# Filtered products of a spectral layer stored by frequency class

## The chip, the core and the metric

The kernel runs on one core of a Trainium2 chip. The metric is the device time of one execution in microseconds, the median of several runs; 204.33 us for the kernel before (204.27 to 204.45 in three runs). A core has five engines with instruction queues of their own, which run side by side and wait for one another through semaphores: TensorE (PE in the profile, with its weight loads as PEld), VectorE (DVE), ScalarE (ACT), GpSimd (POOL) and SyncE (SP, which issues transfers here). SBUF is the on-chip memory of 128 partitions (`arena` in the profile), PSUM the memory that TensorE writes (`ps`).

## What is computed

`x` has 2048 rows of 640 columns in bf16. Cut to what matters:

```python
xn = layernorm(x)                          # over the 640 columns
X = rfft2(xn)                              # 2048 x 321 complex
y = irfft2(X * (w_r + 1j * w_i), s=(2048, 640))
h = (xn @ w_gate) * (xn @ w_up)            # 640 -> 1536
out = x + y + h @ w_down                   # 1536 -> 640
```

One half is a filter in the frequency domain, with a real and an imaginary weight for each frequency; the other is a bilinear gated layer. They share the normalised input and are added at the end.

## The kernel before

The two-dimensional transform is taken apart into small products. The 640 columns fall into ten blocks of 64; butterflies on VectorE (L887 to L925) reduce the ten blocks to five classes of frequencies, and TensorE does the rest with tables. Of the rows, 2048 are 32 times 64: one step over 32 (L938), then, for each of 32 values of `q`, a product over 64. The values of `q` are worked two at a time, in 16 steps of `t`. The way of one `q` through the middle of the kernel is:

- D (L1056): column products, five matmuls of 64 or 65 columns for each half of the pair, evicted to SBUF by ScalarE or VectorE (L718 and L719 are the copy helper that most evictions go through).
- C (L1079): the row product over 64 for one `q`, 128 x 321 in PSUM.
- WM (L1094, L1097): VectorE multiplies the 321 frequencies by `w_r` and `w_i` and writes both products as bf16 into a strip `yg` of SBUF. L1094 runs twice, once for each half (`h`) of classes 0 to 3; 2 weights x 32 frequencies x 4 classes = 256 elements in each. L1097 does class 4 by itself.
- NG (L1106, L1107): the negative of the `w_i` products of classes 0 to 3, on ScalarE, VectorE or GpSimd, as the planner chose (16, 8 and 8 of the 32).
- NS (L1114 to L1116): the copies and the negation for class 4, on GpSimd.
- IA (L1130, L1131): the inverse row product. For each of the five classes, two matmuls of 64 columns that add up in PSUM: first with the weights (`w_r` products, `w_i` products), then with (minus `w_i` products, `w_r` products). Here the filtered products are the stationary operand, so each matmul has a weight load of 128 columns.
- An eviction (L718 or L719), and when all 32 are done the inverse column product I (L1159) with butterflies on VectorE (L1183 to L1216).

Two lines say how `yg` is laid out. WM writes the classes innermost, so that the four classes of one frequency are neighbours, and IA picks one class with a step of four:

```python
dst = yg[:, 578:1090].rearrange("p (w h m k) -> p h w m k", w=2, h=2, k=4)[:, h]
l1, l2 = yg[:, 578 + k:1090:4], yg[:, 322 + k:834:4]
```

Elements 322 to 577 hold minus `w_i` products, 578 to 833 `w_r` products, 834 to 1089 `w_i` products.

The gated layer is woven into this: GU (L978 with 512 columns, L998 with fewer) is five matmuls into a bank of PSUM, evicted mostly by ScalarE, then multiplied by H on VectorE (L1014). The product with `w_down` (L1237), the last step over rows (L1249), and the sum with `x` (L1257) close the kernel.

The order of work is not written by hand: a planner in the kernel takes tasks with estimated durations, priorities and a stock of eight PSUM banks, and fixes one static order for each engine before the program is emitted. Each engine then works through its list in that order and waits where a task needs another engine's result. The estimates belong to the tasks (895 ns for a whole WM, for instance) and not to the access patterns.

Of the kernel before, what the change touches and what calls it, by code (L numbers as in the profile page):

```python
# [495 lines left out]
_ACTF = mybir.ActivationFunctionType  # L496
_OP = AluOpType
# [53 lines left out]
def _build(nc, A_x, A_w_r, A_w_i, B_w_gate, B_w_up, B_w_down, out, opts=None):  # L551
# [3 lines left out]
    with es:  # L555
# [147 lines left out]
        def bank_of(t):  # L703
            return t.units[1]
# [259 lines left out]
        for ui, (at_, ci, ft0) in enumerate(units):  # L964
            b0, nb = chunks[ci][:2]
            n = 128 * nb
# [59 lines left out]
        for t in range(16):  # L1026
            pq = 10.0 + 0.05 * t
            ar = t % 3
            yr = t % _NY
            wr = (t // (_WQ // 2)) % _NW  # L1030
            if t % (_WQ // 2) == 0:
                q0 = 2 * t
                for w_ in range(2):
                    wv, dw = wvs[w_], v_wr[wr][:, w_]
                    parts = [(dw[0:64], wv[:, q0:q0 + _WQ, :].rearrange("k1 q l -> k1 (q l)").unsqueeze(1).to_broadcast(
                        [_S1, 2, _WQ * 321]), 64 * _WQ * 642)]
                    o_ = 0
                    if q0 == 0:
                        o_ = 1
                        parts.append((dw[64:128, 0:321], wv[:, _R // 2, :].unsqueeze(1).to_broadcast([_S1, 2, 321]), 64 * 642))  # L1040
                    for d_ in range(2):
                        parts.append((dw[64 + d_:128:2, 321 * o_:321 * _WQ].rearrange("p (q l) -> p q l", l=321),
                                      wv[:, _R - q0 - o_:_R - q0 - _WQ:-1, :], 32 * (_WQ - o_) * 642))
                    for i_, (dst, src_, nb_) in enumerate(parts):
                        dma("ld_w%d_%d_%d" % (t, w_, i_), dst, src_, nb_,
                            [(b_wr[wr][0], ("r", b_wr[wr][1] + 8 * w_ + 2 * i_, b_wr[wr][1] + 8 * w_ + 2 * i_ + 2))],
                            prio=9.5 + 0.05 * t, semkey=("w", wr), after=[muls[opts.get("w_after", 15)]])

            eds = []
            for w in range(2):  # L1050
                def em_d(c, t=t, w=w):
                    bk = bank_of(c.t)
                    ins = None
                    for k in range(5):
                        n = 64 if k < 4 else 65
                        ins = c.e.matmul(ps[:, bk, k * 64:k * 64 + n], v_uq[:, k, t, :],  # L1056
                                         v_fd[:, k * 128 + w * n: k * 128 + w * n + n], start=True, stop=True)
                    return ins
                td = T("D_%d_%d" % (t, w), "pe", 5 * _d_mm(64), em_d, reads=[(b_u, None), (b_fd, None)],
                       prio=pq, bank="single", cls="b")  # L1060

                def em_ed(c, td=td, ar=ar, w=w):
                    bk = bank_of(td)
                    ins = None
                    for g in range(2):
                        ins = copy_on(c, v_a[64 * w:64 * w + 64, ar, 324 * g:324 * g + 321],
                                      ps[64 * g:64 * g + 64, bk, 0:321])
                    return ins
                ed = T("eD_%d_%d" % (t, w), ("act", "dve"), {"dve": 960.0, "act": 840.0},
                       em_ed, writes=[(b_a, ("r", 2 * ar + w, 2 * ar + w + 1))], prio=pq - 0.001, frees=td)  # L1070
                hold(td, ed)

            for g in range(2):
                q = 2 * t + g
                pg = pq + 0.0005 * g
                ys = 2 * yr + g

                def em_c(c, q=q, g=g, ar=ar):
                    return c.e.matmul(ps[:, bank_of(c.t), 0:_LP], v_tf[:, q, :], v_a[:, ar, 324 * g:324 * g + _LP],  # L1079
                                      start=True, stop=True)  # L1080
                tc = T("C_%d" % q, "pe", _d_mm(_LP), em_c, reads=[(b_a, ("r", 2 * ar, 2 * ar + 2)), (b_tf, ("t", t, t + 1))],
                       prio=pg, bank="single", cls="b")

                def em_wm(c, tc=tc, yr=yr, wr=wr, q=q, g=g):
                    bk = bank_of(tc)
                    o_ = 321 * (q % _WQ)
                    wg = v_wr[wr][:, :, o_:o_ + 321]
                    yg = v_y[:, yr, g]
                    for h in range(2):
                        xh = ps[:, bk, 0:256].rearrange("p (k h m) -> p h m k", k=4, h=2)[:, h]  # L1090
                        wv = wg[:, :, 0:320].rearrange("p w (m k) -> p w m k", k=10)
                        wv = wv[:, :, :, 1:5] if h == 0 else wv[:, :, :, 9:5:-1]
                        dst = yg[:, 578:1090].rearrange("p (w h m k) -> p h w m k", w=2, h=2, k=4)[:, h]
                        c.e.tensor_tensor(dst, xh.unsqueeze(1).to_broadcast([128, 2, 32, 4]), wv, _OP.mult)  # L1094
                    x5 = ps[:, bk, 256:321].unsqueeze(1).to_broadcast([128, 2, 65])
                    d5 = yg[:, 0:512].rearrange("p (w n) -> p w n", w=2)[:, :, 0:65]
                    return c.e.tensor_tensor(d5, x5, wg[:, :, 0:321:5], _OP.mult)  # L1097
                wm = T("WM_%d" % q, "dve", 895.0, em_wm,
                       reads=[(b_wr[wr][0], ("r", b_wr[wr][1], b_wr[wr][1] + 16))],
                       writes=[(b_y, ("r", 4 * ys, 4 * ys + 1))], prio=pg - 0.001, frees=tc)  # L1100
                hold(tc, wm)

                def em_ng(c, yr=yr, g=g):
                    yg = v_y[:, yr, g]
                    if c.e is nc.scalar:
                        return c.e.activation(yg[:, 322:578], yg[:, 834:1090], _ACTF.Copy, scale=-1.0)  # L1106
                    return c.e.tensor_scalar(yg[:, 322:578], yg[:, 834:1090], -1.0, None, _OP.mult)  # L1107
                T("NG_%d" % q, opts.get("ng_eng", ('pool', 'act', 'dve')),
                  {"act": _d_act(256), "dve": _d_dve_ts16(256), "pool": 900.0}, em_ng,
                  reads=[(b_y, ("r", 4 * ys, 4 * ys + 1))], writes=[(b_y, ("r", 4 * ys + 1, 4 * ys + 2))], prio=pg - 0.001)  # L1110

                def em_ns(c, yr=yr, g=g):
                    yg = v_y[:, yr, g]
                    c.e.tensor_copy(yg[:, 65:128], yg[:, 257:320])  # L1114
                    c.e.tensor_copy(yg[:, 193:256], yg[:, 1:64])  # L1115
                    return c.e.tensor_scalar(yg[:, 128:193], yg[:, 256:321], -1.0, None, _OP.mult)  # L1116
                T("NS_%d" % q, "pool", 700.0, em_ns,
                  reads=[(b_y, ("r", 4 * ys, 4 * ys + 1))], writes=[(b_y, ("r", 4 * ys + 2, 4 * ys + 3))], prio=pg - 0.001)

                def em_ia(c, q=q, yr=yr, g=g):  # L1120
                    bk = bank_of(c.t)
                    ins = None
                    yg = v_y[:, yr, g]
                    for k in range(5):
                        if k < 4:
                            l1, l2 = yg[:, 578 + k:1090:4], yg[:, 322 + k:834:4]
                        else:
                            l1, l2 = yg[:, 0:128], yg[:, 128:256]
                        dst = ps[:, bk, 64 * k:64 * k + 64]
                        c.e.matmul(dst, l1, v_ti[:, q, 0, :], start=True, stop=False)  # L1130
                        ins = c.e.matmul(dst, l2, v_ti[:, q, 1, :], start=False, stop=True)  # L1131
                    return ins
                ia = T("IA_%d" % q, "pe", 10 * _d_mm(64), em_ia,
                       reads=[(b_y, ("r", 4 * ys, 4 * ys + 3)), (b_wd, ("e", 128 * q, 128 * q + 128))],
                       prio=pg, bank="single", cls="b")

                def em_eia(c, ia=ia, t=t, g=g):
                    src = ps[:, bank_of(ia), 0:320].rearrange("p (k a m) -> p k a m", k=5, a=16)
                    return copy_on(c, v_z2w[:, :, :, t, 4 * g:4 * g + 4], src)
                eia = T("eIA_%d" % q, ("act", "dve"), {"dve": _d_dve_psum(320), "act": _d_act(320)}, em_eia,  # L1140
                        writes=[(b_z2, ("t", q, q + 1))], prio=pg - 0.001, frees=ia)
                hold(ia, eia)
# [207 lines left out]
```

## Time and profile before

| | |
|---|---|
| device time | 204.33 us (204.27 to 204.45) |
| span in the profile | 202.8 us |
| TensorE busy | 198.0 us (98%), 1785 matmuls |
| VectorE busy | 179.5 us (89%) |
| ScalarE busy | 127.5 us (63%) |
| GpSimd busy | 32.0 us (16%) |
| L1094, 64 instructions | 24.0 us, 416 ns each |
| weight loads of L1130 and L1131, 320 | 23.6 us, 114 and 113 ns each |
| first and last L1094 | 86.5 and 137.1 us |
| first and last L1130 | 90.0 and 139.3 us |

[...]matmuls of 64 columns are listed with 196 ns and start about 30 ns apart. So the pace is read from the starts. Weight loads overlap in the same way. On VectorE, too, an instruction is listed with its tail: two of L1094 in a row take 0.75 us together and not 0.83. A group's row gives line, engine, operation, destination and source with shapes, number of instructions, busy time and mean duration, and the idle time of the engine just ahead of them with what ended it.

### The profile page before, as it was taken

What the parts mean: (1) busy time and instruction counts of PE and PEld (TensorE: products, weight loads), DVE (VectorE), ACT (ScalarE), POOL (GpSimd) and SP (SyncE); (2) the same over time, 40 slices, a digit from 0 to 9 for tenths busy, and PEclk for the clock granted to TensorE, in tenths of its full rate; (3) what the DMA queues carried; (4) which work ended last, traced back from release to release, by engine and by line L of the source; (5) the groups of instructions that cost most, each with busy time, mean ns of one, the idle gap of its engine ahead of it and who ended that gap; (6) DMA issues with size and microseconds to landing.
All of it is one profiled execution on the core that took longest, in us unless ns stands there. A gap on an engine that the chain in (4) does not pass through costs nothing.

```text
span 202.8 us, 4769 instructions
## 1 busy us (share of the span) xinstructions
PE 198.0 (98%) x1785; PEld 128.1 (63%) x1785; DVE 179.5 (89%) x511; ACT 127.5 (63%) x277; POOL 32.0 (16%) x108
## 2 busy tenths in 40 slices
PE   7999999999999999899999999999999999999995
PEld 7987644454444555556666666667777767777774
DVE  3599999999999997697988898864999999999983
ACT  3678899999975776869999999987611220200000
POOL 0000000000000000075754675453000000000000
DMA  6999983031161597605354444004313332332222
GB/s 183 300 341 378 377 80 65 3 65 32 32 63 39 112 276 194 197 14 132 74 145 114 103 102 127 0 5 136 92 32 97 106 107 66 113 90 81 93 65 65
DMA packets 31542, 23.82 MB, mean 117 GB/s; under 512 B 10528, under 2 KB 29472, under 8 KB 31392
## 3 DMA queue, kind: packets, MB, share of 16 engines
q1 hardware_dynamic: 30720, 23.16, 43.5%
q10 hardware_dynamic: 800, 0.36, 0.6%
q8 instruction: 14, 0.23, 0.5%
q14 instruction: 8, 0.07, 0.1%
HBM read 18.92 MB, written 2.62 MB: 106 GB/s over the span
## 4 chain that ended last, share of the span: by engine, by line
PE 85%; DVE 5%; SPq 4%; DMA 4%; issue 1%; ACT 1%
PE ps L978 44%; PE ps L1237 23%; SPq L712 4%; DMA arena<-in_A_x_dram 4%; PE ps L1131 3%; PE ps L1130 3%; PE ps L998 2%; PE ps L1079 2%; PE ps L938 2%; PE ps L1159 2%; PE ps L1249 2%; PE ps L1056 2%; DVE arena L719 1%; DVE arena L1257 1%; DVE arena L1186 0%
## 5 line engine op out<-in xcount | busy, mean ns | idle before, releaser
L718 ACT ACTIVATE arena<-ps 128x512 bf16<-128x512 f32 (+7 forms) x206 | 104.8, 547 | 40.1 <-PE ps L1159 24.0
L978 PE MATMUL ps<-arena 128*128 128x512 bf16 x420 | 97.0, 379 | 0.1
L978 PEld LDWEIGHTS ps<-arena 128*128 128x128 bf16 x420 | 38.9, 98 | 41.9 <-ACT arena L718 1.4
L1237 PE MATMUL ps<-arena 128*128 128x320 bf16 (+2 forms) x396 | 56.5, 295 | 0.2 <-DVE arena L1257 0.2
L1237 PEld LDWEIGHTS ps<-arena 128*128 128x128 bf16 x396 | 37.6, 98 | 13.9 <-DVE arena L1257 0.5
L1094 DVE TENSOR_TENSOR arena<-ps,arena 128x256 bf16<-128x256 f32 x64 | 24.0, 416 | 0.1
L1014 DVE TENSOR_TENSOR arena<-arena 128x512 bf16<-128x512 bf16 x42 | 17.7, 421 | 4.7 <-ACT arena L718 4.7
L1107 POOL TENSOR_SCALAR arena<-arena 128x256 bf16<-128x256 bf16 x8 | 6.8, 855 | 89.3 <-DVE arena L1097 89.2
L719 DVE CAST arena<-ps 64x321 bf16<-64x321 f32 (+1 forms) x25 | 12.2, 490 | 6.3 <-PE ps L1131 5.8
L1257 DVE TENSOR_TENSOR arena<-ps,arena 128x320 bf16<-128x320 f32 (+2 forms) x33 | 15.4, 473 | 1.8 <-PE ps L1249 1.8
L998 PE MATMUL ps<-arena 128*128 128x128 bf16 (+1 forms) x160 | 14.4, 246 | 0.4 <-ACT arena L718 0.4
L1130 PEld LDWEIGHTS ps<-arena 128*128 128x128 bf16 x160 | 12.4, 114 | 2.8 <-ACT arena L718 0.4
L998 PEld LDWEIGHTS ps<-arena 128*128 128x128 bf16 x160 | 12.0, 98 | 2.1 <-ACT arena L718 1.2
L1130 PE MATMUL ps<-arena 128*128 128x64 bf16 x160 | 13.3, 196 | 0.0
L1131 PE MATMUL ps<-arena 128*128 128x64 bf16 x160 | 13.3, 197 | 0.0
L1131 PEld LDWEIGHTS ps<-arena 128*128 128x128 bf16 x160 | 11.2, 113 | 2.1
L1116 POOL TENSOR_SCALAR arena<-arena 128x65 bf16<-128x65 bf16 x32 | 12.1, 378 | 0.0
L1114 POOL COPY arena<-arena 128x63 bf16<-128x63 bf16 x32 | 8.6, 268 | 17.1 <-DVE arena L1097 17.0
L1097 DVE TENSOR_TENSOR arena<-ps,arena 128x130 bf16<-128x130 f32 x32 | 9.3, 292 | 0.0
L776 ACT ACTIVATE arena<-arena 128x640 bf16<-128x640 bf16 x11 | 9.1, 824 | 0.0
L1115 POOL COPY arena<-arena 128x63 bf16<-128x63 bf16 x32 | 9.0, 280 | 0.0
L891 DVE TENSOR_TENSOR arena<-arena 128x384 f32<-128x384 bf16 x16 | 8.8, 552 | 0.0
(62 smaller groups left out, 221.0 us busy)
## 6 DMA issues: line engine op xcount, KB each, us to landing
arena<-in_A_x_dram SPq DMA_DIRECT2D x20, 160.0 KB, 2.4
out_dram<-arena SPq DMA_DIRECT2D x31, 80.0 KB, 1.6
arena<-in_A_w_r_dram SPq DMA_DIRECT2D x8, 160.5 KB, 3.0
arena<-in_A_w_i_dram SPq DMA_DIRECT2D x8, 160.5 KB, 3.0
arena<-in_B_w_gate_dram SPq DMA_DIRECT2D x4, 320.0 KB, 5.8
arena<-in_A_x_dram SPq DMA_DIRECT2D x1, 1280.0 KB, 9.8
arena<-in_A_w_r_dram SPq DMA_DIRECT2D x14, 80.2 KB, 2.9
arena<-in_A_w_i_dram SPq DMA_DIRECT2D x14, 80.2 KB, 3.1
```

What stands on the lines that cost most here:

```text
L718: return c.e.activation(dst, src, _ACTF.Copy)
L719: return c.e.tensor_copy(dst, src)
L978: ins = c.e.matmul(ps[:, bk, :], v_gw[:, w, j, ft, :], v_xt[:, j, rows], start=(j == 0), stop=(j == 4))
L998: ins = c.e.matmul(ps[:, bk, w * n:(w + 1) * n], v_gw[:, w, j, ft, :], v_xt[:, j, rows], start=(j == 0), stop=(j == 4))
L1014: return c.e.tensor_tensor(v_ht[:, ft0, rows], v_gbf[:, rr, 0, :], v_gbf[:, rr, 1, :], _OP.mult)
L1094: c.e.tensor_tensor(dst, xh.unsqueeze(1).to_broadcast([128, 2, 32, 4]), wv, _OP.mult)
L1097: return c.e.tensor_tensor(d5, x5, wg[:, :, 0:321:5], _OP.mult)
L1116: return c.e.tensor_scalar(yg[:, 128:193], yg[:, 256:321], -1.0, None, _OP.mult)
L1130: c.e.matmul(dst, l1, v_ti[:, q, 0, :], start=True, stop=False)
L1131: ins = c.e.matmul(dst, l2, v_ti[:, q, 1, :], start=False, stop=True)
L1237: ins = c.e.matmul(ps[:, bk, 0:sl3.stop - sl3.start], v_ht[:, ft, a * 128:(a + 1) * 128], v_wd[:, ft, sl3], start=(ft == _FT_ORDER[0]), st ...
L1257: return c.e.tensor_tensor(v_out[:, a % 2, sl3], ps[:, bk, 0:sl3.stop - sl3.start], v_xr[:, xs, sl3], _OP.add)
```

## The change

The products of one class are put into one run of columns. The strip from 322 to 1089 keeps its size, but is now four blocks of 192, one for each class `k`, and in each block three runs of 64: minus `w_i` products, `w_r` products, `w_i` products. Both sets of weights of a class are then 128 neighbouring columns of the block, which is what the change is for: the weight load of the inverse row product reads without a step. To get there the products of WM are written with the four classes 192 elements apart, and the negation goes over four rows of 64 in place of one of 256. Class 4 is as it was.

```diff
-                        dst = yg[:, 578:1090].rearrange("p (w h m k) -> p h w m k", w=2, h=2, k=4)[:, h]
+                        dst = yg[:, 322:1090].rearrange("p (k s h m) -> p h s m k", k=4, s=3, h=2)[:, h, 1:3]
                         c.e.tensor_tensor(dst, xh.unsqueeze(1).to_broadcast([128, 2, 32, 4]), wv, _OP.mult)
...
                     yg = v_y[:, yr, g]
+                    yk = yg[:, 322:1090].rearrange("p (k s n) -> p s k n", k=4, s=3)
                     if c.e is nc.scalar:
-                        return c.e.activation(yg[:, 322:578], yg[:, 834:1090], _ACTF.Copy, scale=-1.0)
-                    return c.e.tensor_scalar(yg[:, 322:578], yg[:, 834:1090], -1.0, None, _OP.mult)
+                        return c.e.activation(yk[:, 0], yk[:, 2], _ACTF.Copy, scale=-1.0)
+                    return c.e.tensor_scalar(yk[:, 0], yk[:, 2], -1.0, None, _OP.mult)
...
                         if k < 4:
-                            l1, l2 = yg[:, 578 + k:1090:4], yg[:, 322 + k:834:4]
+                            b0 = 322 + 192 * k
+                            l1, l2 = yg[:, b0 + 64:b0 + 192], yg[:, b0:b0 + 128]
                         else:
                             l1, l2 = yg[:, 0:128], yg[:, 128:256]
```

## The prediction

> **What bounds the kernel now.** I read the chain of waits first, because only work on it can move the end. Over the stretch in which the changed lines run (86 to 137 us), its summary by line is:
>
> ```profile
> by line: PE ps L978 66.0%; PE ps L1131 9.7%; PE ps L1130 9.6%; PE ps L1079 7.5%; PE ps L1056 6.6%; DVE arena L719 1.0%; issue 0.1%
> ```
>
> TensorE holds practically all of it, so here the kernel runs at TensorE's pace; the inverse row product (L1130, L1131), which the change is to speed up, has a fifth of it. But that product's operands come from VectorE, so I next read the busy time of each engine over pieces of about 6.75 us, in which the order of work repeats (two values of t, four of q):
>
> ```profile
> core 0: us, PE busy (x) PEld busy (x) DVE busy (x) ACT busy (x) POOL busy (x), PEclk, DMA share, GB/s
> 85.10:91.95 6.85, 6.83 (x64) 3.98 (x65) 6.78 (x22) 5.09 (x13) 4.37 (x14) 1.00 0.07 19
> 91.95:98.70 6.75, 6.61 (x89) 4.14 (x87) 5.59 (x19) 6.36 (x16) 3.50 (x11) 1.00 0.37 96
> 98.70:105.46 6.76, 6.76 (x90) 4.27 (x87) 5.79 (x20) 6.46 (x16) 3.98 (x14) 1.00 0.58 148
> 105.46:112.20 6.74, 6.74 (x90) 4.25 (x87) 5.80 (x20) 6.49 (x16) 4.02 (x14) 1.00 0.38 100
> ```
>
> VectorE is full in the first piece and idle for only 0.95 us in each later one. That spare time is the number on which the forecast turns. The timeline of VectorE shows where it lies and what stands around it:
>
> ```profile
> 106.83 0.99 DVE L719 CAST arena<-ps 64x321 bf16<-64x321 f32 x2
> 108.73 0.49 DVE L719 CAST arena<-ps 128x320 bf16<-128x320 f32 x1 [0.92 <-PE ps L1131]
> 109.19 0.76 DVE L1094 TENSOR_TENSOR arena<-ps,arena 128x256 bf16<-128x256 f32 x2
> 109.87 0.30 DVE L1097 TENSOR_TENSOR arena<-ps,arena 128x130 bf16<-128x130 f32 x1
> 110.08 0.42 DVE L1014 TENSOR_TENSOR arena<-arena 128x512 bf16<-128x512 bf16 x1
> ```
>
> The only gap is one wait of 0.92 us for an inverse product; everything else on VectorE stands shoulder to shoulder. Last, the groups by shape give the durations:
>
> ```profile
> L1094 DVE TENSOR_TENSOR arena<-ps,arena 128x256 bf16<-128x256 f32 x64 | 24.0, 416 | 0.1
> ...
> L1130 PEld LDWEIGHTS ps<-arena 128*128 128x128 bf16 x160 | 12.4, 114 | 2.8 <-ACT arena L718 0.4
> ...
> L1097 DVE TENSOR_TENSOR arena<-ps,arena 128x130 bf16<-128x130 f32 x32 | 9.3, 292 | 0.0
> ...
> L1056 PEld LDWEIGHTS ps<-arena 128*128 128x128 bf16 x160 | 6.5, 98 | 0.7 <-issue 0.2
> ```
>
> A weight load with a step of four elements takes 114 ns on average, one without a step 98.
>
> **What the Trainium skill says.** (1) "Vector Engine (DVE) Microarchitecture Reference", section "5.2 Measured stream behaviour on trn2 (trn3 not measured)": a port keeps its full rate only while elements come in runs of at least two adjacent words; a destination that hops 4 KiB at every element takes 1.71 ns per column in place of 1.054, one that steps 24 words takes 2.50, and two sources that step 72/152 words take 1.75. These are for 4-byte data. No long instruction in the trace of before writes SBUF one element at a time, so it doesn't show this; it shows that runs are free (the 320-element copy on VectorE that writes runs of four bf16 took 492 ns, the 64 products 416, the same as float32 instructions of 256 elements with long runs, 415 to 421). It also speaks partly against a strict reading: L1097 reads bf16 at a step of 10 bytes, each mostly alone in its 8 bytes, and at 292 ns shows no visible penalty. (2) "SBUF — State Buffer", section "Door 1: The DMA port swizzle": lines of 16 bytes, with at least two hits in a line needed for full rate; L1097 has 1.6 a line, the new writes one. (3) "VectorE: DVE Perf Modes", section "Mode 1× (REGULAR) — the baseline": the plain mode takes "weird strides, PSUM operands — all work". The trace agrees for a PSUM source read at a step of 256 bytes (L1094 today). (4) "TensorE: Matmul & The Clock Gate", section "LDWEIGHTS (loading the stationary operand)": the time follows the number of columns. The trace differs, 114 against 98 ns at 128 columns; the measurement decides.
>
> **The change part by part.** The number and order of instructions is the same on every engine; only access patterns change, so no wait is added by the program.
>
> *The weight loads of L1130 and L1131, four of five classes.* I summed all blocks of inverse products in TensorE's timeline, start to start: 10.36 us for 320 matmuls, 32.4 ns each. The column product L1056, as narrow but with weights in one run, goes at 0.29 us for ten, 29.2 each. The change makes every block like that: 320 x 3.2 ns = 1.0 us less for TensorE, 0.13 us in each piece of 6.75. All of it is on today's path.
>
> *The products of L1094, 64 instructions of 256 elements.* The inner four elements of the destination, today adjacent (8 bytes), are put 384 bytes apart (192 elements of bf16), so each lands alone; sources and element count are unchanged. Cost per element, bounded from both sides: nothing (the trace shows no penalty for single bf16 reads at 10 bytes) up to 2.50 - 1.05 = 1.45 ns (the 24-word step). I take 1.71 - 1.054 = 0.656 ns, because that price is for a destination that goes round a few regions and returns to the next element of each, as ours goes round four classes; 256 x 0.656 = 168 ns, L1094 at some 584. An estimate, from the page's table.
>
> *The negation (L1106/L1107: 16 on ScalarE, 8 on VectorE at 250 ns, 8 on GpSimd at 855).* Its 256 elements become four rows of 64, each in one run and at an even offset. I cost it at nothing on all three, since rows of 64 are long runs.
>
> *L1097, the zero-frequency class and its copies on GpSimd (L1114 to L1116)* are untouched.
>
> **What the 168 ns do.** Behind each L1094 on VectorE stand further products, H (L1014), the negations and the evictions of L719; TensorE waits for products through the negation (0.25 to 0.86 us) and the copies on GpSimd (0.86 us together), with 0.4 to 1.1 us to spare (read off the timelines of the three engines between 104 and 112 us) before the inverse product has to start. First run of twelve (86.5 to 91.9): 12 x 0.168 = 2.0 us, less gaps of 0.30 and 0.85 up to 95.7: 0.9 late. Six pieces up to 136: each gets 8 x 0.168 = 1.34 us and has 0.95: 0.39 x 6 = 2.35 late. The last four products have 0.67 more just ahead of the last inverse products and little slack: 0.4. Sum 3.7 us. TensorE's 1.0 us gain lies in the same stretch, and there it only becomes waiting, since VectorE now sets the pace. Everything after 139 us starts later by the same amount: the butterflies of the inverse transform wait for the last inverse product, and their stage (VectorE holds the chain from 156 to 164 us) is unchanged. 204.3 + 3.7 = 208.0 us.
>
> **The rivals.** *R1, scattered writes are free, or cheap enough to hide.* For it: L1097's reads at 10 bytes and L1094's PSUM reads at 256 bytes run at full rate. Up to about 100 ns per product would vanish in the gaps ((0.30 + 0.85 + 6 x 0.95) / 60 = 0.11 us for the first 60). Then TensorE keeps its gain: 204.3 - 1.0 = 203.3. ScalarE, 6.49 of 6.74 us busy, could cap it, but 0.13 us per piece is within its 0.25 of spare time. Against it: one hit per line, which both pages price. *R2, the penalty is a whole cycle or more per element.* At one cycle (1.04 ns, an estimate between the two prices): 267 ns per product; 12 x 0.267 - 1.15 = 2.05, six times (2.13 - 0.95) = 7.1, last 0.9: 10 us, 214.4. At 2.50 ns per column: 372 ns; 3.3 + 12.2 + 1.3 = 16.8 us, 221.1. For it: the write is of two bytes, and our 384 bytes are nearer to the 24-word step than 4 KiB is. Against: the 72/152-word steps cost hardly more than 4 KiB. *R3, the penalty exists but TensorE and VectorE share it well:* the gaps take it almost wholly and gain and loss cancel, within 0.2% of before.
>
> **How the numbers follow.** Forecast 0.50; R1 0.22; R2 0.26, half of it at or below the one-cycle case; R3 0.02. The range goes from 203.2 (R1 at its full gain) to 214.5 (the one-cycle case) and leaves out the upper half of R2 and a little more, under 0.2. Faster is R1, 0.22, same is R3 with edges, 0.03, slower the rest, 0.75.
>
> **What would show it.** The mean of L1094: 584 ns is the forecast, 416 is R1, 680 or more R2. The weight loads of L1130 and L1131 should stand at 98 ns in every case, and blocks of ten inverse products at 0.29 us where TensorE doesn't wait. In the forecast VectorE has no gap left between 86 and 137 us, its wait for L1131 is gone, the pieces of 6.75 us grow to about 7.15, and TensorE's products wait for GpSimd, ScalarE or VectorE. I am wrong if L1094 does not move (then the pieces shrink to about 6.62), or if rows of 64 slow the negations.

## The result and the profile after

The changed kernel takes 251.49 us (250.16 to 252.7), beside 204.39 us for the kernel before on the same chip: a ratio of 1.230 (95% interval 1.225 to 1.234), 47.1 us slower. The direction of the forecast was right and its size far off.

The chain of waits from 83 to 140 us of the changed kernel (line numbers above L1097 have moved by up to two):

```profile
by line: DVE arena L1094 69.2%; DVE arena L719 10.1%; issue 6.2%; DVE arena L1014 4.1%; PE ps L978 3.9%; DVE arena L1097 3.7%; PE ps L1056 1.7%; PE ps L1132 0.9%; PE ps L1133 0.9%; DVE arena L1108 0.6%; PE ps L1079 0.3%
```

VectorE has taken the path over from TensorE, and over two thirds of it are the products. The groups by shape:

```profile
L1094 DVE TENSOR_TENSOR arena<-ps,arena 128x256 bf16<-128x256 f32 x64 | 78.2, 1413 | 1.5 <-PE ps L1079 1.4
...
L1097 DVE TENSOR_TENSOR arena<-ps,arena 128x130 bf16<-128x130 f32 x32 | 16.1, 504 | 0.0
...
L1132 PEld LDWEIGHTS ps<-arena 128*128 128x128 bf16 x160 | 12.0, 104 | 35.3 <-ACT arena L718 19.2 <-issue 7.6 <-DVE arena L1014 3.4
...
L1107 ACT ACTIVATE arena<-arena 128x256 bf16<-128x256 bf16 x16 | 6.7, 417 | 39.9 <-DVE arena L1097 39.9
```

L1094 went from 416 to 1413 ns. L1097 was not touched and is listed with 504 in place of 292: it starts at 108.34 in the timeline below, before the two products ahead of it end (106.27 + 2.46 = 108.73), so a listed duration tells less than the step from start to start. That step is in the same timeline of VectorE:

```profile
105.66 0.49 DVE L719 CAST arena<-ps 128x320 bf16<-128x320 f32 x1 [2.03 <-PE ps L1133]
106.27 2.46 DVE L1094 TENSOR_TENSOR arena<-ps,arena 128x256 bf16<-128x256 f32 x2
108.34 0.51 DVE L1097 TENSOR_TENSOR arena<-ps,arena 128x130 bf16<-128x130 f32 x1
108.76 0.41 DVE L1014 TENSOR_TENSOR arena<-arena 128x512 bf16<-128x512 bf16 x1
```

Two L1094 and one L1097, all the products of one q, take 108.76 - 106.27 = 2.49 us; in the lines of before it is 110.08 - 109.19 = 0.89. With 0.21 for L1097, one L1094 takes 1.14 us of VectorE's time (before 0.34): 0.80 us more, 3.1 ns for each of 256 elements. Before, an element took about 1.05 ns, an estimate: 0.34 us for the 256 of L1094 and 0.21 for the 130 of L1097 make 0.13 us for 126 elements, and some 70 ns are left for each instruction. A lone bf16 so comes to about 4.2 ns in all.

Busy time of the engines in pieces of four q, which now last 12.25 us in place of 6.75:

```profile
core 0: us, PE busy (x) PEld busy (x) DVE busy (x) ACT busy (x) POOL busy (x), PEclk, DMA share, GB/s
101.00:106.27 5.27, 4.39 (x43) 2.87 (x44) 3.11 (x8) 2.47 (x6) 0.87 (x3) 0.54 0.15 35
106.27:118.55 12.28, 7.84 (x86) 4.10 (x85) 12.23 (x19) 6.93 (x16) 4.04 (x13) 1.00 0.21 54
118.55:130.78 12.23, 7.61 (x85) 4.07 (x84) 12.19 (x20) 6.71 (x16) 4.04 (x13) 1.00 0.33 83
```

In the second and third row VectorE has no gap left (12.23 of 12.28), and TensorE is busy for less than two thirds. In the first row the granted clock of TensorE is 0.54, and it works at about half speed: in the chain, five matmuls of L978 take 2.23 us there, 1.08 before. That has a part in VectorE's wait of 2.03 us for L1133 at 105.66. The same wait before was shorter:

```profile
95.23 0.49 DVE L719 CAST arena<-ps 128x320 bf16<-128x320 f32 x1 [0.85 <-PE ps L1131]
```

What lowers the clock there no run isolates.

### The profile page after: what moved, and what is told of

The parts are those of the page before. It is cut to its first block, busy times and chain, and to the rows that moved or that the text cites. A ratio compares the mean times of both kernels' runs of the same rounds, so it can differ in the third digit from the quotient of the medians.

```text
span 249.8 us, 4769 instructions
## 1 busy us (share of the span) xinstructions
PE 212.2 (85%) x1785; PEld 130.4 (52%) x1785; DVE 230.4 (92%) x511; ACT 129.0 (52%) x277; POOL 32.7 (13%) x108
## 4 chain that ended last, share of the span: by engine, by line
PE 50%; DVE 37%; issue 4%; SPq 3%; DMA 3%; POOL 1%; ACT 1%; POOLq 0%
DVE arena L1094 27%; PE ps L978 23%; PE ps L1239 19%; DVE arena L719 4%; SPq L712 3%; DMA arena<-in_A_x_dram 3%; PE ps L998 2%; PE ps L938 2%; DVE arena L1014 2%; PE ps L1161 2%; DVE arena L1097 2%; PE ps L1251 2%; PE ps L1056 1%; PE ps L1132 0%; POOL arena L1117 0%
## 5 line engine op out<-in xcount | busy, mean ns | idle before, releaser
L978 PE MATMUL ps<-arena 128*128 128x512 bf16 x420 | 104.2, 399 | 7.0 <-DVE arena L1097 6.9
L1094 DVE TENSOR_TENSOR arena<-ps,arena 128x256 bf16<-128x256 f32 x64 | 78.2, 1413 | 1.5 <-PE ps L1079 1.4
L978 PEld LDWEIGHTS ps<-arena 128*128 128x128 bf16 x420 | 40.2, 101 | 53.6 <-DVE arena L1097 8.6
L1239 PEld LDWEIGHTS ps<-arena 128*128 128x128 bf16 x396 | 37.6, 98 | 13.9 <-DVE arena L1259 0.5
L1132 PE MATMUL ps<-arena 128*128 128x64 bf16 x160 | 14.9, 202 | 24.2 <-ACT arena L718 12.0
L1132 PEld LDWEIGHTS ps<-arena 128*128 128x128 bf16 x160 | 12.0, 104 | 35.3 <-ACT arena L718 19.2
L1107 ACT ACTIVATE arena<-arena 128x256 bf16<-128x256 bf16 x16 | 6.7, 417 | 39.9 <-DVE arena L1097 39.9
L1259 DVE TENSOR_TENSOR arena<-ps,arena 128x320 bf16<-128x320 f32 (+2 forms) x33 | 16.3, 500 | 1.8 <-PE ps L1251 1.8
L1097 DVE TENSOR_TENSOR arena<-ps,arena 128x130 bf16<-128x130 f32 x32 | 16.1, 504 | 0.0
L1115 POOL COPY arena<-arena 128x63 bf16<-128x63 bf16 x32 | 9.3, 291 | 50.7 <-DVE arena L1097 50.7
L1133 PE MATMUL ps<-arena 128*128 128x64 bf16 x160 | 14.9, 202 | 0.0
L719 DVE CAST arena<-ps 64x321 bf16<-64x321 f32 (+1 forms) x25 | 12.2, 490 | 2.6 <-PE ps L1133 2.0
L998 PEld LDWEIGHTS ps<-arena 128*128 128x128 bf16 x160 | 12.0, 98 | 2.1 <-ACT arena L718 1.2
L1133 PEld LDWEIGHTS ps<-arena 128*128 128x128 bf16 x160 | 11.9, 104 | 0.8 <-issue 0.8
L1056 PE MATMUL ps<-arena 128*128 128x64 bf16 (+1 forms) x160 | 8.7, 201 | 1.7 <-DVE arena L1097 1.7
```

The costliest lines, as they stand in the source:

```text
L719: return c.e.tensor_copy(dst, src)
L978: ins = c.e.matmul(ps[:, bk, :], v_gw[:, w, j, ft, :], v_xt[:, j, rows], start=(j == 0), stop=(j == 4))
L998: ins = c.e.matmul(ps[:, bk, w * n:(w + 1) * n], v_gw[:, w, j, ft, :], v_xt[:, j, rows], start=(j == 0), stop=(j == 4))
L1239: ins = c.e.matmul(ps[:, bk, 0:sl3.stop - sl3.start], v_ht[:, ft, a * 128:(a + 1) * 128], v_wd[:, ft, sl3], start=(ft == _FT_ORDER[0]), st ...
L1259: return c.e.tensor_tensor(v_out[:, a % 2, sl3], ps[:, bk, 0:sl3.stop - sl3.start], v_xr[:, xs, sl3], _OP.add)
```

## Experiments

The theory from here on: the write of one bf16 far from its neighbours is what costs. The rivals: the order of the walk or the number of levels in the pattern, a bad pitch of 384 bytes, and, within the theory, what about the lone write is dear.

**The other order of the walk.** The layout stays; m is innermost, and the weights are read at a step of 20 bytes.

```diff
-"p (k s h m) -> p h s m k"    # destination; sources alike
+"p (k s h m) -> p h s k m"
```

> The class-run layout of the changed kernel, but L1094 walks its 256 elements with the frequency index innermost and the class outside it: runs of 32 adjacent bf16 are written, and the weights are read at a step of 20 bytes instead. Instruction count, patterns of three levels, layout and weight loads as in the changed kernel. Theory A (what costs 1413 ns is the lone two-byte write): L1094 back to 416 to 430 ns, time 203.0 to 203.8 us, since the weight loads keep the gain of 1.0 us. Theory B (a pattern with three levels or any hop on any port costs): L1094 at 580 ns or more and 208 us or more.

Measured: 210.74 us, ratio 1.030 (1.029 to 1.032); L1094 at 608 ns, the weight loads of L1132 and L1133 at 97 and 98.

```profile
106.14 1.14 DVE L1094 TENSOR_TENSOR arena<-ps,arena 128x256 bf16<-128x256 f32 x2
107.20 0.29 DVE L1097 TENSOR_TENSOR arena<-ps,arena 128x130 bf16<-128x130 f32 x1
107.40 0.61 DVE L1094 TENSOR_TENSOR arena<-ps,arena 128x256 bf16<-128x256 f32 x1
```

A q takes 1.26 us, one L1094 (1.26 - 0.21) / 2 = 0.525, which is 0.185 more than before, or 0.72 ns for each of 256 elements: 1.77 in all. Neither theory was right in full. The instruction has as many levels as in the changed kernel and loses most of the penalty, so it is not the shape; but reading lone bf16 at 20 bytes has a price of its own, those 0.72 ns an element, where L1097's reads at 10 bytes show none. The Trainium skill, "Vector Engine (DVE) Microarchitecture Reference", section "5.2 Measured stream behaviour on trn2 (trn3 not measured)", has 1.73 ns for one source that hops 4 KiB at every element, for 4-byte data; this read of 2-byte elements at 20 bytes comes out near it.

**The gain of the weight loads alone.**

```diff
-l1, l2 = yg[:, 578 + k:1090:4], yg[:, 322 + k:834:4]
+l1, l2 = yg[:, 578 + 128 * k:706 + 128 * k], yg[:, 322 + 128 * k:450 + 128 * k]
```

> The kernel before with one edit: the inverse row product loads its weights from 128 adjacent columns of the old layout, so its classes are mixed and the output is not the reference's; VectorE, ScalarE and GpSimd are as before. It shows the gain of the weight loads alone. Theory A: loads of L1130 and L1131 at 98 ns, blocks of ten inverse products at 0.29 us, 203.3 us (1.0 us less). Rival: TensorE's pace is set by ScalarE or by other waits and the time stays at 204.2 to 204.5.

Measured: 203.92 us, ratio 0.9968 (0.9956 to 0.9981), so 0.65 us less (0.4 to 0.9) where 1.0 was expected.

```profile
L1130 PEld LDWEIGHTS ps<-arena 128*128 128x128 bf16 x160 | 11.0, 98 | 2.9 <-ACT arena L718 0.5
```

In the timeline of VectorE the pieces of 6.75 us became 6.62 to 6.63, the 0.13 us each that were forecast. From the first L1097 to the first eviction of the inverse column product the two profiles differ by 0.93 us (53.99 before, 53.06 here); the profiled run of this kernel came 0.27 us later to that first L1097, over work that the edit does not touch. The chain of this kernel between 86 and 138 us:

```profile
by line: PE ps L978 62.9%; PE ps L1130 8.5%; PE ps L1079 8.3%; PE ps L1131 8.1%; PE ps L1056 5.7%; ACT arena L718 3.5%; issue 1.3%; DVE arena L719 1.0%; ACT arena L1106 0.6%; PE ps L1237 0.3%
```

ScalarE's evictions, absent from this chain before, now have 3.5% of it; whether they hold back a part of the gain is not shown. Even with free writes the change could have won little more than this.

**Another pitch.**

```diff
-b0 = 322 + 192 * k
+b0 = 322 + 200 * k            # and the writes to match
```

> The changed kernel with the class blocks 200 elements (400 bytes) apart in place of 192 (384 bytes); nothing else. Theory A1 (any lone two-byte write costs the same): L1094 within 5% of 1413 ns, about 251 us. Theory A2 (384 bytes is a multiple of 128, so that the four writes of a group meet in one bank): L1094 at 600 ns or less and 203 to 210 us.

Measured: 249.49 us, ratio 1.220 (1.217 to 1.222); L1094 is 2% from the changed kernel's.

```profile
L1094 DVE TENSOR_TENSOR arena<-ps,arena 128x256 bf16<-128x256 f32 x64 | 76.5, 1383 | 1.4 <-PE ps L1079 1.4
```

The pitch of 384 bytes is not the cause.

**Lone float32.**

```diff
+if h == 0:
+    dst = yg[:, 322:1090].bitcast(_F32).rearrange("p (k s m) -> p s m k", k=4, s=3)[:, 0:2]
+    c.e.tensor_tensor(dst, xh.unsqueeze(1).to_broadcast([128, 2, 32, 4]), wv, _OP.is_gt)
```

> The changed kernel, but of the two instructions of L1094 the one for h = 0 writes float32 elements at the same 384 bytes from element to element (a comparison in place of the product, at the same element count), and the one for h = 1 writes bf16 in runs of 32 into the rest of each block; the output is not the reference's. Theory A1a (the two-byte write is the dear one, since it fills only half of a 4-byte word): the float32 instruction at 585 to 800 ns[...]. Theory A1b (a lone write of any size costs): about 1400 ns. Theory A2 (banks): about 1400 ns as well, since the pitch is the same. The bf16 instruction at about 416 ns in all.

Measured: 207.56 us, ratio 1.015 (1.013 to 1.016).

```profile
L1095 DVE TENSOR_TENSOR arena<-ps,arena 128x256 f32<-128x256 f32 x32 | 19.4, 607 | 0.1
L1098 DVE TENSOR_TENSOR arena<-ps,arena 128x256 bf16<-128x256 f32 x32 | 19.0, 593 | 0.0
```

```profile
106.26 0.61 DVE L1095 TENSOR_TENSOR arena<-ps,arena 128x256 f32<-128x256 f32 x1
106.71 0.60 DVE L1098 TENSOR_TENSOR arena<-ps,arena 128x256 bf16<-128x256 f32 x1
```

The float32 instruction (L1095) makes the same hops and takes 607 ns. It starts 0.45 us before its successor, 0.11 more than L1094 before: 0.11 us / 256 = 0.43 ns on top of 1.05, 1.48 ns an element. It is the width that makes the write dear. The second row, forecast at 416, has the reads at 20 bytes of the first experiment, and their price.

**Two halves of one word, or half a word.** In the changed kernel the write four elements later fills the other half of the same 4-byte word. Here it can't.

```diff
-"p (k s h m) -> p h s m k"
+"p (k s m h) -> p h s m k"
```

> The changed kernel with one edit: in a class block the two halves h lie interleaved (m outside, h inside), so the elements that one instruction of L1094 writes never share a 4-byte word; each is still a lone two-byte write, 384 bytes from the one before. The weights of a class come out in another order, so the output is not the reference's. Theory P (a lone two-byte write costs by itself, since it fills half a word): L1094 within 10% of 1413 ns, about 250 us. Theory H (the cost is a conflict between two writes to the halves of one word, four elements apart): L1094 at about 600 ns, as the lone float32 write, and 206 to 213 us.

Measured: 251.81 us, ratio 1.230 (1.225 to 1.236).

```profile
L1094 DVE TENSOR_TENSOR arena<-ps,arena 128x256 bf16<-128x256 f32 x64 | 78.1, 1411 | 1.7 <-PE ps L1079 1.7
```

No conflict between neighbours: the hopping half word costs as much when its word's other half is left alone.

**Pairs.** Two classes side by side, hopping pairs of 4 bytes.

```diff
-"p (k s h m) -> p h s m k", k=4, s=3, h=2
+"p (a s h m b) -> p h s m a b", a=2, s=3, h=2, b=2      # one instruction for each w
...
-l1, l2 = yg[:, b0 + 64:b0 + 192], yg[:, b0:b0 + 128]
+l1, l2 = yg[:, b0 + 128:b0 + 384 - k % 2:2], yg[:, b0:b0 + 256 - k % 2:2]
```

> The changed kernel with two classes side by side: element pairs (4 bytes, starting on a word) hop from block to block, and the weight loads step by two elements. [...]L1094 becomes two instructions of 128 elements. Both theories on the half word: a pair fills a word, so at most 0.73 ns per element for the hop over words in place of 4.3: about 210 to 330 ns for 128 elements, 204 to 211 us. If any hop, whatever it fills, costs 4.3 ns per element or more than 2 ns, 340 to 630 ns and over 215 us. The weight loads at a step of two: 98 if only the step of four was slow, else 105 to 114.

> As e6_pairs, with the whole strip moved by one element, so that every pair straddles two 4-byte words. Theory P: each element is a half-word write again, 128 x 4.3 + 75, some 600 to 700 ns per instruction and 245 us or more. Theory H: the same, if the two halves of a word come from pairs written close together. Rival (only hops count, words don't): the same as e6_pairs within 5%.

Measured, on a word: 204.37 us, ratio 0.9988 (0.9980 to 0.9996). Off the word: 223.06 us, ratio 1.090 (1.086 to 1.094). From the groups of the first and of the second, then the timelines of VectorE in the first and the second, with the products of one q each (in these two kernels L1095 are the products of classes 0 to 3 and L1098 those of class 4):

```profile
L1095 DVE TENSOR_TENSOR arena<-ps,arena 128x128 bf16<-128x128 f32 x128 | 28.1, 282 | 0.1
...
L1133 PEld LDWEIGHTS ps<-arena 128*128 128x128 bf16 x160 | 10.9, 98 | 4.5 <-ACT arena L1108 1.6 <-ACT arena L718 0.8 <-issue 0.4
```

```profile
L1095 DVE TENSOR_TENSOR arena<-ps,arena 128x128 bf16<-128x128 f32 x128 | 50.5, 572 | 0.6 <-PE ps L1079 0.6
```

```profile
105.91 0.87 DVE L1095 TENSOR_TENSOR arena<-ps,arena 128x128 bf16<-128x128 f32 x4
106.71 0.29 DVE L1098 TENSOR_TENSOR arena<-ps,arena 128x130 bf16<-128x130 f32 x1
106.92 0.41 DVE L1014 TENSOR_TENSOR arena<-arena 128x512 bf16<-128x512 bf16 x1
```

```profile
106.51 1.58 DVE L1095 TENSOR_TENSOR arena<-ps,arena 128x128 bf16<-128x128 f32 x4
107.84 0.38 DVE L1098 TENSOR_TENSOR arena<-ps,arena 128x130 bf16<-128x130 f32 x1
108.14 0.40 DVE L1014 TENSOR_TENSOR arena<-arena 128x512 bf16<-128x512 bf16 x1
```

On a word, four instructions take 0.80 us, 0.20 each, which is what 128 elements in plain order would take (128 x 1.05 + 70 ns): a hopping pair is free. One element further (108.14 - 106.51 = 1.63 us for a q, less 0.21, a fourth of it 0.355) each takes 0.155 us more: with 64 pairs, 2.4 ns more a pair, which at 2.1 ns for its two elements makes 4.5. That is nearly what a lone bf16 costs (4.2). So by these figures the price goes with each visit to a place that is left with a half-filled word, and not with each element. The expectation put it on each element: the listed 572 ns are near its 600 to 700, since they contain the delay of the writes ahead, but its 245 us and more were too much. And a step of two, 4 bytes, loads weights at full rate (98 ns), where a step of four took 114.

**Pairs, written in a row.**

```diff
-for w in range(2):    # dst[:, w], both pairs
+for a in range(2):    # dst[:, :, :, a], both weights
```

> The layout of e6_pairs, but each instruction of 128 elements takes one pair of classes, so it writes 64 adjacent elements in a row, and only the weights are read in hopping pairs. A version that could win: if pair reads are free (210 ns from start to start), VectorE gets 0.17 us more for each q, 0.68 in a piece of 6.75 us with 0.95 to spare, and the weight loads keep up to 0.65 us: 203.7 to 204.3 us. If pairs read at 20 bytes cost as the lone reads of e1_m_inner do (1.76 ns per element, 300 ns from start to start), VectorE gets 0.53 us more for each q, and it is slower: 209 to 213 us.

Measured: 204.81 us, ratio 1.0006 (0.9997 to 1.0014), above the 203.7 to 204.3 expected for free reads.

```profile
L1095 DVE TENSOR_TENSOR arena<-ps,arena 128x128 bf16<-128x128 f32 x128 | 28.7, 289 | 0.1
```

A q takes 1.02 us in the timeline, so pair reads at 20 bytes are almost free. The timelines also show where the gain of the weight loads goes, in much the same way in both pair layouts. The first six q, in which VectorE has little idle time, take 9.68 us (9.61 with hopping pairs, 9.19 before), counted from the first product of class 4 to the seventh; the 24 q after them take 39.97 (39.82, and 40.23 before). Here L1095 has 30.6% of the chain between 86 and 137 us, and with hopping pairs VectorE has none, though it is busy for 6.37 us of the piece from 105.46 to 112.20 in both (5.80 before). What makes the two differ by 0.4 us is not shown.

**Half words with no hop.**

```diff
-"p (w h m k) -> p h w m k"    # in the kernel before
+"p (w m k h) -> p h w m k"
```

> The kernel before with one edit: L1094 writes its elements in the old order of classes, but at a step of two elements, the halves h interleaved, so each element fills half of a word and the next element half of the next word; nothing hops. The order of the products differs, so the output is not the reference's; the rest is as before, the weight loads with their step of four included. Theory P1 (each half-filled word costs about 4 ns, wherever the next one is): L1094 at about 1400 ns, 250 us. Theory P2 (the cost is paid for each visit to a line or a pair of words, as the straddling pairs of e7_pairs_off_word hint, at 4 ns for two elements): half of that or less, 420 to 800 ns, 204 to 225 us.

Measured: 204.88 us, ratio 1.0004 (0.9990 to 1.0018).

```profile
L1094 DVE TENSOR_TENSOR arena<-ps,arena 128x256 bf16<-128x256 f32 x64 | 24.9, 443 | 0.1
```

Each element again fills half a word, and it is nearly free (443 for 416 ns). So a half-filled word alone isn't dear either; it takes the half word and the hop together. One reading that fits all runs is a price of about 4 ns for each visit to a small stretch of memory that leaves a word half filled, paid in parallel with the elements that arrive in that visit: one element (the changed kernel) or two (pairs off the word) leave much of it open, more elements in a row cover it. No run isolates this, or shows how long such a stretch is, why a half-filled word costs, or from which distance between 4 and 384 bytes on it does.

## Why the prediction was right and wrong

- **TensorE's pace in this stage, and VectorE's spare 0.95 us in each piece:** right (the second piece shown has 1.16, the two gaps of 0.30 and 0.85). The products of a q, their time and the result go together: 0.12 and 0.14 us more per q (both pair layouts) are within 0.95 / 4 = 0.24 and did not lengthen the pieces; they cost 0.4 to 0.5 us in the first six q. 0.37 more (the other order) cost 6.2 us.
- **Weight loads:** 97 or 98 ns, as forecast, in the five experiments with faster loads and a clock of 1.00; 104 in the changed kernel, with a mean clock of 0.952, where L1056, which nobody touched, went from 98 to 103. The 0.13 us in each piece was right. In all the loads are worth 0.65 us alone (0.4 to 0.9) and not 1.0. The first six q, in which VectorE has little idle time, became shorter by only 0.08 us (9.11 for 9.19); the rest of the difference is open.
- **Negations:** right; ScalarE 417 ns before and after, VectorE 250 and 261, GpSimd 855 and 853.
- **The price of the write, 0.656 ns an element:** this term failed. It is a price for 4-byte elements, taken over to 2-byte ones; so was the upper bound, 1.45. The prediction said that its prices were for 4-byte data, and under R2 that the write is of two bytes, but it gave the width no term of its own. The lone float32 run comes out near the price of the Trainium skill, "Vector Engine (DVE) Microarchitecture Reference", section "5.2 Measured stream behaviour on trn2 (trn3 not measured)", for that width: 1.48 ns in all, below its 1.71. The lone bf16 costs 4.2 ns, 3.1 more than in plain order, above both ends. What was forecast as 168 ns more for each L1094 was 0.80 us.
- **What L1097 was taken to say** (lone 2-byte accesses at 10 bytes are free) holds for that read only: reads at 20 bytes cost 0.72 ns, writes 3.1.
- **The sum:** fed with what was measured, 1.60 us more per q, the scheme gives 44 of the measured 47.1 us. First run, six q: 9.6 - 1.15 = 8.4. Six pieces: 6 x (6.4 - 0.95) = 32.7. The last two q: 3.2 less 0.27 of slack, 2.9. The timelines of VectorE show 10.6 (from the first L1094 to the thirteenth, 9.18 us before and 19.74 after), then 33.3 and 3.1. So most of what is missing lies in the first run, where a second and smaller step failed: VectorE's gap of 0.85 us ahead of L719 was counted as absorbed, and it grew to 2.03. The granted clock of 0.54 is not the whole cause, for in the runs with the other order and with lone float32, both at a clock of 1.00, 0.73 us of the gap stayed. What part the clock has no run isolates. Fed with the 0.37 us of the other order, the scheme is short as well: it gives 4.7 of 6.2 us.
- **R2** named the right side, but with 2.50 ns as the worst case it ended at 221.1 us; with bounds from 4-byte data the range could not hold the time.

One version is ahead of both kernels: pairs on a word, by 0.12% against before (0.04 to 0.20), with the full rate of weight loads paid for by 64 more instructions on VectorE. It is small, and less than the 0.32% that the weight loads give alone.

## What to carry to other kernels

Before a layout is changed for the reader's sake, look at what the writer's innermost elements become: here pairs of bf16 that fill a 4-byte word could be scattered for nothing, and single bf16 cost 3.1 ns more each. A price for a pattern holds for the element width it was measured at, and where the width differs it is no bound. Ask first how much idle time the writing engine has between the waits of the engine on the path (here 0.24 us per q), and compare it with the most the reader can gain (here 0.65 us in all).

## What the runs showed that was not expected

- A lone bf16 written 384 or 400 bytes from the last costs VectorE about 4.2 ns (L1094 at 1413 and 1383 ns), a lone float32 at 384 bytes 1.48, a pair of bf16 that fills a word nothing extra, a pair that straddles two words about 4.5 for the pair.
- Single bf16 at a step of 4 bytes are written at nearly full rate (443 for 416 ns).
- Weight loads of bf16 are as fast with a step of two elements as with none (98 ns), and not with four (114 ns on average over a mix with loads of step one).
- An instruction behind such writes is listed with their delay: L1097 at 504 ns for 292, though its own work was the same.
